# One two-bank PSUM tile for both heads' scores, one VectorE instruction over it, and a new order for the attention and first feed-forward stages

## The chip, the cores and the metric

The kernel runs on one core of one Trainium2 chip. The metric is the device time of one execution in microseconds (us). The core's engines work in parallel from queues of their own: TensorE (PE; PEld is its weight load), VectorE (DVE), ScalarE (ACT), GpSimd (POOL) and SyncE (SP), which here only issues DMAs.

## What is computed

Four batches of 576 tokens with 8 heads of 64. Each head has a pooled ("global") attention over groups of four tokens and a local one over a band of seven; their sum, 2304 tokens by 512, goes through two feed-forward stages:

```python
out_d = sm_attn(q_d, k_d, v_d)            # q, k, v averaged over 4 tokens
out_up = np.repeat(out_d, 4, axis=2)
scores = np.where(np.abs(i - j) < 4, scale * q @ k.T, -1e9)
x = out_up + softmax(scores) @ v          # per head, then heads side by side
h = np.maximum(np.maximum(x @ w1, x @ w2), x @ w3)   # 512 -> 768
x = h @ w_out                                        # 768 -> 512
h = x @ w_in                                         # 512 -> 2048
out = np.maximum(0.01 * h, h) @ w_out2               # 2048 -> 512
```

## The kernel before, in words

All matrices of the feed-forward stages are split into a high and a low part, and each product is three matmuls (high by high, high by low, low by high).

**Units.** The 2304 tokens are eight units of 288 (`NU`, `NCOL`), two per batch. A unit needs its input X (high `xh`, low `xl`); then `L1_mm` makes 18 products of 12 matmuls each (six column blocks by three weights, `ps_h`), `L1_max` keeps the maximum of three (`hm`), `L1_hh` (ScalarE) and `L1_hl` (GpSimd) split it, and `L2_mm` makes four products of 18 matmuls (`ps_o`). Phase 2 (`L3`, `L4`) is the second feed-forward stage; nothing of it is touched.

**Local attention** comes in two ways. For units 0 to 3 (`pairs`) the scores are made by PE for two heads at a time: step C writes two PSUM tiles `ps_ls` (a band mask, then six matmuls), D (VectorE) takes maxima and scales them, E (ScalarE) is six exponentials with sums, H (VectorE) adds an epsilon and inverts, I (GpSimd) normalises, O (PE) transposes into `ps_lt`, o (VectorE) copies to `plt`, P (PE) multiplies by v, Q (VectorE) adds the pooled part (`x`), R (ScalarE) and S (GpSimd) split into X. For units 4 to 7 VectorE, GpSimd and ScalarE do it without PE, each unit in two halves: three products on GpSimd (`qkprod`, line 371), reductions, a mask added on GpSimd (line 391), a subtraction of the maximum on VectorE (line 402), an exponential, a division, three products with v (`pvprod`, line 425) and sums. In unit 4 the probabilities `lp` lie in SBUF, in units 5 to 7 in PSUM (lines 397 to 400). `turn_steps` then transposes the result (`ps_x`), adds the pooled part and splits it into X.

**Pooled attention** (`ds_` steps): A sums groups of four, B is PE's scores `ps_sc` in two tiles, F, G, J, K are the softmax like D, E, H, I; M transposes into two tiles `ps_aT`, m (ScalarE) copies them, N (PE) multiplies by the pooled v (PV, GpSimd), v (ScalarE) copies the result to `up`.

**Weights** of the first stage, 18 `wA` and 6 `wO`, arrive as 64-bit numbers and are converted in four steps: x (ScalarE, lines 304 and 305), y (VectorE, 307 and 310), z (ScalarE, 316) and u (GpSimd, 318). Two work tiles `wy` serve them all. L1 of unit 0 waits for the `wA` one by one, the `ps_o` products for the `wO`.

**The order** is fixed by the program on every engine, and an engine takes its instructions one after the other. The string `ORDER` is the first part, batch 0's attention for unit 0 (each letter a step above, the digit a head pair or a weight); `ps0`, a PSUM pool of eight banks, serves it, with small matmuls on a zero tile `warm` (`fill`) between. From there to the end of phase 1 the class `Plan` sets the order: a list schedule with a cost for each step, due times made from `LEN` (one length per unit) and shifted by kind with `SHIFT`, and a window in which a step may begin (`SLACK`). Its PSUM pools are `mm` (four banks), `at` (two) and `early` (two); `holds` tells it which step takes a buffer and which gives it back.

Of the kernel before, what the change touches and what calls it, by code (L numbers as in the profile page):

```python
# [56 lines left out]
FILL1 = 8  # L57
ON_A = (0, 21, 14)
# [6 lines left out]
SHIFT = {'pv': 31, 'ra': 0, 't': -48, 'mu': 73, 'c': 15, 'ds3': 4, 'ds2': -60, 'pl3': -19, 'pl1': 4}  # L65
SLACK = {'ds1': 100, 'pl3': 150, 'ds3': 30, 'ra': 150, 'pv': 60, 'ds2': 60, 'c': 20, 'mu': 150}
LEN = (64, 78, 40, 47, 39, 56, 39, 39)
# [123 lines left out]
def local_global_attention_moe_kernel(  # L191
# [61 lines left out]
    PS = {"0": tc.alloc_tile_pool(name="ps0", bufs=7, space=PSUM)}  # L253
# [226 lines left out]
    def pl_C(u, h):  # L480
        qr, kr = pl[u, h, "q"], pl[u, h, "k"]
        n = NBLK * KB
        pst = pl[u, h, "ps"] = [scratch(u, "early", "ps_ls") for hh in range(2)]
        if u == 0:
            fill("C", pst[0])
        for t in pst:
            T.matmul(
                out=t[:QB, :n], lhsT=ident_b, rhs=bands[u % 2].rearrange("p n k -> p (n k)"), start=True, stop=False
            )
        for j in range(NBLK):  # L490
            s0 = u % 2 * NCOL + j * QB
            qs, ks = slice(s0, s0 + QB), slice(s0, s0 + KB)
            for hh in range(2):
                rows = slice(64 * hh, 64 * hh + 64)
                T.matmul(  # L495
                    out=pst[hh][:QB, j * KB : j * KB + KB], lhsT=qr[rows, qs], rhs=kr[rows, ks],
# [3 lines left out]
    def pl_D(u, h):  # L500
# [3 lines left out]
        st = pl[u, h, "st"] = [  # L504
            stats[:QB, 24 * h + 6 * hh : 24 * h + 6 * hh + 6] if u == 0 else pst[hh][:QB, n : n + 6] for hh in range(2)
        ]
        for hh in range(2):
            ps = pst[hh][:QB, :n].rearrange("p (n k) -> p n k", n=NBLK)
            V.tensor_reduce(out=st[hh][:, :NBLK], in_=ps, axis=AX.X, op=ALU.max, negate=True)
            V.tensor_scalar(out=nm[:, hh], in0=st[hh][:, :NBLK], scalar1=SCALE, scalar2=None, op0=ALU.mult)  # L510

    def pl_E(u, h):
        n = NBLK * KB
# [7 lines left out]
        for hh in range(2):  # L521
            ps = pst[hh][:QB, :n].rearrange("p (n k) -> p n k", n=NBLK)
            for j in range(NBLK):
                A.activation(  # L524
                    out=et[:, hh, j], in_=ps[:, j], func=AF.Exp, scale=SCALE,
                    bias=nm[:, hh, j : j + 1], accum_out=sm[:, hh, j : j + 1],
                )

    def pl_H(u, h):
        st, sm = pl.pop((u, h, "st")), pl[u, h, "sum"]  # L530
        pl.pop((u, h, "ps"))
        for hh in range(2):
# [8 lines left out]
    def pl_O(u, h):  # L541
        pts = []
        for n, (j0, j1) in enumerate(((0, 2), (2, 3))):
            pt = scratch(u, "at", "ps_lt")
            if u == n == 0:
                fill("O", pt)
            pt = pt[:KB, : (j1 - j0) * 2 * QB].rearrange("p (j h q) -> p j h q", h=2, q=QB)
            for j in range(j0, j1):
                for hh in range(2):
                    T.transpose(out=pt[:, j - j0, hh], in_=pl[u, h, "e"][:, hh, j], identity=ident[:QB, :QB])  # L550
            pts.append(pt)
        pl[u, h, "pt"] = pts
# [747 lines left out]
```

## Time and profile before

| | us |
|---|---|
| median of 3 runs | 841.9 (840.14 to 841.92) |
| the profiled execution | 840.65 |
| its span, first to last instruction | 838.9 |
| PE busy | 809.9 (97%) |
| VectorE, ScalarE, GpSimd busy | 458.0, 401.4, 254.1 |

The profiled execution's time is its span and 1.75 us around it. Lines named L and a number are lines of the kernel before. A time such as 105.02 is counted from the span's start; "a <-b" means that a is written from b. "idle before <-X" says how long the engine stood still and whose work ended that. The view of stretches gives each engine's busy time in a part of the span.

### The profile page before, as it was taken

What the parts mean: (1) busy time and instruction counts of PE and PEld (TensorE: products, weight loads), DVE (VectorE), ACT (ScalarE), POOL (GpSimd) and SP (SyncE); (2) the same over time, 40 slices, a digit from 0 to 9 for tenths busy, and PEclk for the clock granted to TensorE, in tenths of its full rate; (3) what the DMA queues carried; (4) which work ended last, traced back from release to release, by engine and by line L of the source; (5) the groups of instructions that cost most, each with busy time, mean ns of one, the idle gap of its engine ahead of it and who ended that gap; (6) DMA issues with size and microseconds to landing.
All of it is one profiled execution on the core that took longest, in us unless ns stands there. A gap on an engine that the chain in (4) does not pass through costs nothing.

```text
span 838.9 us, 13935 instructions
## 1 busy us (share of the span) xinstructions
PE 809.9 (97%) x5124; PEld 706.6 (84%) x5128; DVE 458.0 (55%) x894; ACT 401.4 (48%) x1451; POOL 254.1 (30%) x237
## 2 busy tenths in 40 slices
PE   7889599989999999999999999999999999999997
PEld 3569499879999999999998888888888888888896
DVE  6769845588886874939509982422232223322332
ACT  5878937678375565137418972322232222322222
POOL 6768749789864792111100000000000000000000
PEclk9989799999999999999999999999999999999999
DMA  9781333435313131242029400300030001000100
GB/s 274 284 341 51 104 119 104 153 125 172 121 52 132 58 88 46 83 135 96 22 73 392 166 0 1 101 0 1 1 101 0 1 1 53 23 1 1 39 13 25
DMA packets 28100, 74.49 MB, mean 89 GB/s; under 512 B 3648, under 2 KB 9152, under 8 KB 28032
## 3 DMA queue, kind: packets, MB, share of 16 engines
q1 hardware_dynamic: 23232, 68.62, 24.1%
q10 hardware_dynamic: 4800, 4.98, 1.7%
q8 instruction: 40, 0.66, 0.3%
q14 instruction: 28, 0.23, 0.1%
HBM read 64.16 MB, written 9.44 MB: 88 GB/s over the span
## 4 chain that ended last, share of the span: by engine, by line
PE 87%; DVE 4%; ACT 4%; DMA 3%; issue 1%; POOL 1%; SPq 0%; ACTq 0%; DVEq 0%; POOLq 0%
PE ps_h L802 26%; PE ps_g L899 24%; PE acc L923 24%; PE ps_o L834 9%; ACT qkprod L385 2%; DMA wA<-in_wa_dram 1%; DMA dsrawv<-in_vP_dram 1%; PE ps_up L717 1%; PE ps_sc L643 1%; DVE lp L402 1%; DVE wl L307 1%; PE ps_aT L695 1%; PE ps_ls L495 1%; PE ps_lo L572 1%; ACT ple L524 1%
## 5 line engine op out<-in xcount | busy, mean ns | idle before, releaser
L802 PE MATMUL ps_h<-xh,wA 128*128 128x288 f32 x1152 | 199.7, 301 | 1.9 <-ACT xh L591 1.8
L923 PE MATMUL acc<-w2o,gh 128*128 128x512 f32 x576 | 177.9, 391 | 0.0
L802 PEld LDWEIGHTS ps_h<-xh,wA 128*128 128x128 f32 x1152 | 167.7, 189 | 7.4 <-issue 2.3
L907 DVE TENSOR_TENSOR g<-g,ps_g 128x512 f32<-128x512 f32 (+1 forms) x80 | 50.7, 634 | 199.7 <-ACT g L906 199.6
L899 PE MATMUL ps_g<-x2h,w2i 128*128 128x512 f32 (+1 forms) x640 | 159.0, 370 | 0.1
L906 ACT ACTIVATE g<-ps_g 128x512 f32<-128x512 f32 (+1 forms) x80 | 44.5, 556 | 200.7 <-PE ps_g L899 200.7
L899 PEld LDWEIGHTS ps_g<-x2h,w2i 128*128 128x128 f32 x640 | 114.6, 188 | 23.3 <-ACT ev L841 0.3
L923 PEld LDWEIGHTS acc<-w2o,gh 128*128 128x128 f32 x576 | 107.0, 188 | 22.0
L923 PE MATMUL acc<-w2o,gl 128*128 128x512 f32 x288 | 112.0, 391 | 0.0
L802 PE MATMUL ps_h<-xl,wA 128*128 128x288 f32 x576 | 109.4, 296 | 0.5 <-POOL xl L594 0.5
L802 PEld LDWEIGHTS ps_h<-xl,wA 128*128 128x128 f32 x576 | 88.3, 189 | 0.7 <-POOL xl L594 0.7
L834 PE MATMUL ps_o<-hh,wO 128*128 128x288 f32 x384 | 81.4, 306 | 0.0
L899 PE MATMUL ps_g<-x2l,w2i 128*128 128x512 f32 (+1 forms) x320 | 79.6, 370 | 0.0
L371 POOL TENSOR_TENSOR qkprod<-lq,lk 128x1344 f32<-128x1344 f32 x24 | 73.8, 3081 | 6.5 <-ACT qkprod L385 3.7
L825 POOL TENSOR_TENSOR hl<-hm,hh 128x288 fp32r<-128x288 f32 x48 | 41.3, 861 | 108.3 <-ACT hh L821 108.0
L818 DVE TENSOR_TENSOR hm<-hm,ps_h 128x288 f32<-128x288 f32 x96 | 43.3, 451 | 56.3 <-PE ps_h L802 51.3
L911 DVE TENSOR_TENSOR gl<-g,gh 128x512 fp32r<-128x512 f32 (+1 forms) x80 | 51.0, 638 | 39.6 <-ACT gh L910 35.6
L385 ACT ACTIVATE qkprod<-qkprod 128x64 f32<-128x64 f32 x280 | 67.4, 250 | 3.8 <-POOL qkprod L371 2.8
L910 ACT ACTIVATE gh<-g 128x512 fp32r<-128x512 f32 (+1 forms) x80 | 47.0, 588 | 42.2 <-DVE g L907 41.8
L899 PEld LDWEIGHTS ps_g<-x2l,w2i 128*128 128x128 f32 x320 | 56.8, 188 | 10.9
L834 PEld LDWEIGHTS ps_o<-hh,wO 128*128 128x128 f32 x384 | 62.9, 193 | 2.0 <-issue 1.6
L923 PEld LDWEIGHTS acc<-w2o,gl 128*128 128x128 f32 x288 | 54.1, 188 | 11.8
(129 smaller groups left out, 1110.6 us busy)
## 6 DMA issues: line engine op xcount, KB each, us to landing
sqk<-in_qk_dram SPq DMA_DIRECT2D x20, 579.0 KB, 4.2
wA<-in_wa_dram SPq DMA_DIRECT2D x18, 512.0 KB, 10.5
w2i<-in_w_in_dram SPq DMA_DIRECT2D x16, 512.0 KB, 6.0
w2o<-in_w_out_dram SPq DMA_DIRECT2D x16, 512.0 KB, 8.5
dsrawv<-in_vP_dram SPq DMA_DIRECT2D x16, 320.0 KB, 4.2
x2d<-ev ACTq DMA_DIRECT2D x32, 144.0 KB, 1.7
raw<-x2d SPq DMA_DIRECT2D x16, 256.0 KB, 3.9
lk<-in_kL_dram SPq DMA_DIRECT2D x8, 480.0 KB, 4.1
```

The lines of the kernel that those rows point to most:

```text
L371: P.tensor_tensor(out=pr, in0=in0, in1=in1, op=ALU.mult)
L385: A.activation(out=pr[:, r, j], in_=pr[:, r, j], func=AF.Copy, accum_out=sc[:, r, j : j + 1])
L802: T.matmul(out=ps, lhsT=wA[m, e][wi][:, kk * 128 : kk * 128 + 128], rhs=xx[:, kk] if u < PEU else xx[:, :, kk, :], start=n == 0, stop=n == ...
L818: V.tensor_tensor(out=hmax[u, m], in0=hmax[u, m], in1=ps, op=ALU.max)
L825: P.tensor_tensor(out=hl[:, m], in0=hmax[u, m], in1=hh[:, m].bitcast(F32), op=ALU.subtract)
L834: T.matmul(out=ps, lhsT=wO[m][wi][:, os_], rhs=xx[:, m], start=m == n == 0, stop=m == M1 - 1 and n == 2)
L899: T.matmul(out=ps, lhsT=w2i[m][wi][:, kk * 128 : kk * 128 + 128], rhs=xx[:, kk, :n], start=j == 0, stop=j == 3 * KC - 1,)
L906: A.activation(out=g, in_=ps, func=AF.Copy, scale=0.01)
L907: V.tensor_tensor(out=g, in0=g, in1=ps, op=ALU.max)
L910: A.activation(out=gh, in_=g, func=AF.Copy)
L911: V.tensor_tensor(out=gl, in0=g, in1=gh.bitcast(F32), op=ALU.subtract)
L923: T.matmul(out=accs[c, t], lhsT=a[:, ts], rhs=w, start=m == 0 and j == 0, stop=m == M2 - 1 and j == 2)
```

## The change

Wherever a step used two one-bank PSUM tiles for two heads (or two halves), it now uses one tile of two banks, and the VectorE or ScalarE instructions that read them work on both banks at once: D, H, F and J have two instructions instead of four, o and m one instead of two. N moves from the `at` pool to `mm`. `turn_steps` takes the nine rows of a unit in groups of eight and one, where it took three groups. `ORDER` is a new string, and `SHIFT`, `SLACK`, `LEN` and the plan's costs are new, so that phase 1 is ordered anew. Eight matmuls on the zero tile (`FILL2`) stand in unit 0's first product, ahead of the part that needs the last head pair.

```diff
 ORDER = (
-    "C0 A0 A1 B0 L0 D0 C1 A2 E0 F0 L1 B1 H0 G0 D1 I0 C2 J0 E1 F1 K0 A3 L2 G1 M0 D2 x0 O0 J1 m0 L3 y0 "
...
+    "C0 A0 A1 L0 B0 D0 C1 A2 E0 F0 L1 B1 H0 G0 D1 I0 A3 E1 C2 F1 L2 x0 H1 O0 J0 D2 G1 K0 y0 E2 L3 B2 o0 J1 "
...
+FILL2 = 8
...
-LEN = (64, 78, 40, 47, 39, 56, 39, 39)
+LEN = (58, 68, 44, 42, 51, 58, 39, 40)
...
     def scratch(first, kind, name):
...
-            return PS["0"].tile([128, 512], F32, tag=tag, bufs=6 if tag == "b" else 1, name=name)
-        return PS[kind].tile([128, 512], F32, tag=kind, name=name)
+            if tag == "b":
+                return PS["0"].tile([128, 2, 512], F32, tag=tag, bufs=3, name=name)
+            return PS["0"].tile([128, 512], F32, tag=tag, bufs=1, name=name)
+        return PS[kind].tile([128, 512] if kind == "mm" else [128, 2, 512], F32, tag=kind, name=name)
...
     def pl_D(u, h):
...
-        for hh in range(2):
-            ps = pst[hh][:QB, :n].rearrange("p (n k) -> p n k", n=NBLK)
-            V.tensor_reduce(out=st[hh][:, :NBLK], in_=ps, axis=AX.X, op=ALU.max, negate=True)
-            V.tensor_scalar(out=nm[:, hh], in0=st[hh][:, :NBLK], scalar1=SCALE, scalar2=None, op0=ALU.mult)
...
+        V.tensor_reduce(
+            out=st[:, :, :NBLK], in_=pst[:QB, :, :n].rearrange("p h (n k) -> p h n k", n=NBLK), axis=AX.X,
+            op=ALU.max, negate=True,
+        )
+        V.tensor_scalar(out=nm, in0=st[:, :, :NBLK], scalar1=SCALE, scalar2=None, op0=ALU.mult)
...
     def pl_H(u, h):
...
+        V.tensor_scalar(out=st[:, :, NBLK : 2 * NBLK], in0=sm, scalar1=1e-9, scalar2=None, op0=ALU.add)
+        V.reciprocal(out=sm, in_=st[:, :, NBLK : 2 * NBLK])
...
     def pl_o(u, h):
...
-        for (j0, j1), pt in zip(((0, 2), (2, 3)), pl.pop((u, h, "pt"))):
-            V.tensor_copy(out=t[:, j0:j1], in_=pt)
+        V.tensor_copy(out=t, in_=pl.pop((u, h, "pt"))[:KB, :, :NCOL])
...
     def ds_N(b, h):
-        ps = scratch(b, "at", "ps_up")
+        ps = scratch(b, "mm", "ps_up")
...
     def turn_steps(u):
...
-        groups = ((0, 3), (3, 7), (7, 9)) if half and not whole else ((0, 4), (4, 8), (8, 9))
+        groups = ((0, 8), (8, 9))
...
     def L1_mm(u, m, e):
...
         for n, (wi, xx, kk) in enumerate(order):
+            if u == m == e == 0 and n == 3 * (KC - 1):
+                fill("", PS["early"].tile([128, 2, 512], F32, tag="early", name="warm_ps"), FILL2)
...
-        PS["at"] = p1.enter_context(tc.tile_pool(name="ps_at", bufs=2, space=PSUM, reuse_waits="tile"))
-        PS["early"] = tc.alloc_tile_pool(name="ps_early", bufs=2, space=PSUM, reuse_waits="tile")
+        PS["at"] = p1.enter_context(tc.tile_pool(name="ps_at", bufs=1, space=PSUM, reuse_waits="tile"))
+        PS["early"] = tc.alloc_tile_pool(name="ps_early", bufs=1, space=PSUM, reuse_waits="tile")
```

D, H, F, J, ds_B, ds_M, pl_C and pl_O change alike: the index of the head becomes the tile's second dimension. Three places of the new order follow.

**VectorE, end of batch 0.** `x32` is step Q of the second, third and fourth head pair, `plt` step o, `wl3` and `wy` the two halves of a conversion's step y; the names `wA1_1` and so on say which weight. Before:

```order
L307 SCALAR_TENSOR_TENSOR wl3_611<-wA0_1_150,wl3_611 128x512
L310 SCALAR_TENSOR_TENSOR wy_610<-wy_610,wl3_611 128x512
L585 TENSOR_TENSOR x32_647<-ps_lo_618,up_410 128x288
L560 COPY plt_661<-ps_lt_635 102x384
L560 COPY plt_661<-ps_lt_642 102x192
L307 SCALAR_TENSOR_TENSOR wl3_650<-wA2_0_166,wl3_650 128x512
L310 SCALAR_TENSOR_TENSOR wy_649<-wy_649,wl3_650 128x512
L585 TENSOR_TENSOR x32_684<-ps_lo_667,up_410 128x288
L307 SCALAR_TENSOR_TENSOR wl3_681<-wA1_2_164,wl3_681 128x512
```

Now:

```order
L310 SCALAR_TENSOR_TENSOR wl3_571<-wA0_2_156,wl3_571 128x512
L313 SCALAR_TENSOR_TENSOR wy_570<-wy_570,wl3_571 128x512
L559 COPY plt_600<-ps_lt_580 102x576
L586 TENSOR_TENSOR x32_620<-ps_lo_605,up_432 128x288
L310 SCALAR_TENSOR_TENSOR wl3_617<-wA1_0_160,wl3_617 128x512
L313 SCALAR_TENSOR_TENSOR wy_616<-wy_616,wl3_617 128x512
L310 SCALAR_TENSOR_TENSOR wl3_629<-wA2_1_168,wl3_629 128x512
L313 SCALAR_TENSOR_TENSOR wy_628<-wy_628,wl3_629 128x512
L310 SCALAR_TENSOR_TENSOR wl3_636<-wA2_0_166,wl3_636 128x512
```

The last Q had six conversions ahead of it and has five now; the copy is one instruction.

**PE, unit 0's first product and the first C of unit 1.** `ps_h` is the product, `warm_ps` the new small matmuls, `ps_ls` step C; the brackets name the semaphores that a row waits for. Before:

```order
L802 MATMUL ps_h<-xh,wA_0_393 128x288 [waits Activation_49]
L802 MATMUL ps_h<-xl,wA_0_393 128x288 [waits Pool_49]
L802 MATMUL ps_h<-xh,wA_0_393 128x288
L487 LDWEIGHTS ident_b
L487 MATMUL ps_ls<-band,ident_b 96x306 [waits PE_49]
L487 LDWEIGHTS ident_b
L487 MATMUL ps_ls<-band,ident_b 96x306 [waits DVE_49]
L495 MATMUL ps_ls<-sqk 96x102 x6
L802 MATMUL ps_h<-xh,wA_1_645 128x288
```

Now (the pair of `warm` rows comes eight times):

```order
L803 MATMUL ps_h<-xh,wA_0_421 128x288
L289 LDWEIGHTS warm [waits DVE_49]
L289 MATMUL warm_ps<-warm 128x512 [waits Activation_49]
L289 LDWEIGHTS warm
L289 MATMUL warm_ps<-warm 128x512
...
L803 MATMUL ps_h<-xh,wA_0_421 128x288 [waits Activation_49]
L803 MATMUL ps_h<-xl,wA_0_421 128x288 [waits Pool_49]
L803 MATMUL ps_h<-xh,wA_0_421 128x288
L490 LDWEIGHTS ident_b
L490 MATMUL ps_ls<-band,ident_b 96x306 [waits PE_49]
```

VectorE's step that C's second bank waited for is the eighth conversion's y (of weight `wA2_1`). The small matmuls wait for the eighth conversion's y now too (of `wA2_0`), because their tile has both banks, and the last three matmuls of the product stand behind them.

**GpSimd, around unit 4's second mask addition** (`ls`). `qkprod` are the products of local attention, `ple` step I, `xl` step S, `hl` the split of h. Before:

```order
L391 TENSOR_TENSOR ls<-ls,mask_66 128x21
L825 TENSOR_TENSOR hl<-hm,hh 128x288
L539 TENSOR_TENSOR ple<-ple,plsm 96x612
L391 TENSOR_TENSOR ls<-ls,mask_66 128x21
L594 TENSOR_TENSOR xl<-x_2244,xh 128x288
L371 TENSOR_TENSOR qkprod<-lq,lk 128x1344 x2
```

Now:

```order
L541 TENSOR_TENSOR ple<-ple,plsm 96x612
L394 TENSOR_TENSOR ls<-ls,mask_66 128x21
L374 TENSOR_TENSOR qkprod<-lq,lk 128x1344 x2
L826 TENSOR_TENSOR hl<-hm,hh 128x288
L595 TENSOR_TENSOR xl<-x_2159,xh 128x288
L541 TENSOR_TENSOR ple<-ple,plsm 96x612
L374 TENSOR_TENSOR qkprod<-lq,lk 128x1344
```

The two products that follow the second mask addition stood one S behind it and now stand right behind it.

## Rows read from the trace of the kernel before

**Rows 1.** The page: busy time of each engine, share of the span, instructions.

```profile
PE 809.9 (97%) x5124; PEld 706.6 (84%) x5128; DVE 458.0 (55%) x894; ACT 401.4 (48%) x1451; POOL 254.1 (30%) x237
```

**Rows 2.** Busy time in three stretches (windows), by engine, with granted clock.

```profile
core 0: us, PE busy (x) PEld busy (x) DVE busy (x) ACT busy (x) POOL busy (x), PEclk, DMA share, GB/s
45.70:102.10 56.40, 44.02 (x350) 39.18 (x349) 46.03 (x119) 48.26 (x152) 40.09 (x37) 0.86 0.46 168
88.30:105.00 16.70, 8.18 (x75) 6.12 (x75) 14.26 (x45) 14.56 (x51) 11.79 (x11) 0.65 0.24 83
436.80:838.90 402.10, 396.98 (x1824) 328.94 (x1824) 155.98 (x251) 141.14 (x252) 0.00 (x0) 1.00 0.14 51
```

**Rows 3.** Waits of PE: total us, times, longest us.

```profile
PE ps_ls L487 <- DVE ps_ls L534: 5.6, 1, 5.6
PE ps_up L717 <- DVE plt L560: 3.1, 1, 3.1
PE ps_ls L487 <- DVE wy L310: 1.6, 1, 1.6
```

**Rows 4.** Timeline of PE, 17 to 51 us: start, us, instruction, idle before.

```profile
17.87 3.42 PE L286 MATMUL warm_ps<-warm 128*128 128x512 bf16 x8
50.88 0.41 PE L487 MATMUL ps_ls<-band,ident_b 96*96 96x306 bf16 x1 [1.63 <-DVE wy L310]
```

**Rows 5.** Chain of waits, fifteen equal matmuls, three stretches: start, us, what.

```profile
105.02 3.01 PE ps_o L834 x15
172.27 3.47 PE ps_o L834 x15
261.17 2.00 PE ps_o L834 x15
```

**Rows 6.** Groups of VectorE instructions by shape: count, busy us, mean ns, idle before.

```profile
L381 DVE TENSOR_REDUCE ls<-qkprod 128x21 f32<-128x1344 f32 x8 | 12.2, 1544 | 0.0
L509 DVE TENSOR_REDUCE ps_ls<-ps_ls 96x3 f32<-96x306 f32 x24 | 11.4, 473 | 4.5 <-PE ps_ls L495 4.5
L560 DVE COPY plt<-ps_lt 102x384 f32<-102x384 f32 x16 | 8.8, 551 | 6.6 <-PE ps_lt L550 4.5 <-POOL dsvaT L475 2.1
L381 DVE TENSOR_REDUCE ls<-qkprod 128x7 f32<-128x448 f32 x8 | 4.9, 614 | 3.9 <-POOL qkprod L371 3.9
L510 DVE TENSOR_SCALAR plnm<-ps_ls 96x3 f32<-96x3 f32 x24 | 3.8, 157 | 0.8
L310 DVE SCALAR_TENSOR_TENSOR wy<-wy,wl 128x512 int32<-128x512 int32 x56 | 39.6, 708 | 2.9
```

**Rows 7.** Timeline of VectorE in the first batch and at the last conversions.

```profile
24.55 0.82 DVE L560 COPY plt<-ps_lt 102x384 f32<-102x384 f32 x2 [2.09 <-POOL dsvaT L475]
45.24 0.45 DVE L585 TENSOR_TENSOR x<-ps_lo,up 128x288 f32<-128x288 f32 x1
...
101.41 0.69 DVE L310 SCALAR_TENSOR_TENSOR wy<-wy,wl 128x512 int32<-128x512 int32 x1
```

**Rows 8.** Timeline of ScalarE: end of a conversion, one begun, six exponentials.

```profile
84.19 0.62 ACT L316 ACTIVATE wA<-wy 128x512 fp32r<-128x512 f32 x1
84.71 0.66 ACT L304 ACTIVATE wy<-wO 128x512 f32<-128x512 f32 x1
85.82 0.34 ACT L524 ACTIVATE ple<-ps_ls,plnm 96x102 f32<-96x102 f32 x1
87.75 0.67 ACT L304 ACTIVATE wy<-wO 128x512 f32<-128x512 f32 x1
```

**Rows 9.** GpSimd: the fifth output-weight conversion; the two products at 161.74.

```profile
103.16 1.28 POOL L318 TENSOR_TENSOR wO<-wy,wO 128x512 fp32r<-128x512 f32 x1 [0.71 <-ACT wO L316]
...
161.74 6.07 POOL L371 TENSOR_TENSOR qkprod<-lq,lk 128x1344 f32<-128x1344 f32 x2
```

**Rows 10.** VectorE line L402's and L425's durations: min/median/max ns.

```profile
L402 DVE TENSOR_TENSOR lp<-ls,lp x8: 225/228/6598, 159.5 to 327.8; 128x63 f32<-128x63 f32 x8
...
L425 DVE TENSOR_TENSOR pvprod<-lp,lv x24: 1532/1550/2712, 176.8 to 350.5; 128x1344 f32<-128x1344 f32 x24
```

More of the change, by code (lines that the diff above doesn't have):

```diff
@@ L495, in pl_C @@
                 T.matmul(
-                    out=pst[hh][:QB, j * KB : j * KB + KB], lhsT=qr[rows, qs], rhs=kr[rows, ks],
+                    out=pst[:QB, hh, j * KB : j * KB + KB], lhsT=qr[rows, qs], rhs=kr[rows, ks],
                     start=False, stop=j == NBLK - 1,
@@ L541, in pl_O @@
     def pl_O(u, h):
[L542 to L552, printed above, removed]
+        pt = scratch(u, "at", "ps_lt")
+        if u == 0:
+            fill("O", pt)
+        for j in range(NBLK):
+            for hh in range(2):
+                T.transpose(
+                    out=pt[:KB, hh, j * QB : j * QB + QB], in_=pl[u, h, "e"][:, hh, j], identity=ident[:QB, :QB]
+                )
+        pl[u, h, "pt"] = pt
     def pl_o(u, h):
         if u == 0:
-            t = late_tile([KB, NBLK, 2, QB], "plt")
+            t = late_tile([KB, 2, NCOL], "plt")
         else:
-            t = pools[u // 2].tile([KB, NBLK, 2, QB], F32, tag="plt", bufs=1, name="plt")
-        for (j0, j1), pt in zip(((0, 2), (2, 3)), pl.pop((u, h, "pt"))):
-            V.tensor_copy(out=t[:, j0:j1], in_=pt)
+            t = pools[u // 2].tile([KB, 2, NCOL], F32, tag="plt", bufs=1, name="plt")
+        V.tensor_copy(out=t, in_=pl.pop((u, h, "pt"))[:KB, :, :NCOL])
         pl[u, h, "aT"] = t
@@ L636, in ds_B @@
         t = dst[b, h, "qk"]
-        pst = dst[b, h, "ps"] = [scratch(b, "at", "ps_sc") for hh in range(2)]
+        pst = dst[b, h, "ps"] = scratch(b, "at", "ps_sc")
         if b == 0:
-            fill("B", pst[0])
+            fill("B", pst)
         for c in range(2):
@@ L675, in ds_J @@
         dst.pop((b, h, "ps"))
[L676 to L679 removed]
+        sm = sum4.rearrange("p (h n) -> p h n", h=2)
+        V.tensor_scalar(out=st[:, :, 2:4], in0=sm, scalar1=1e-9, scalar2=float(FAC), op0=ALU.add, op1=ALU.mult)
+        V.reciprocal(out=sm, in_=st[:, :, 2:4])
     def ds_norm(b, h):
@@ L1021, in pairs @@
             go(f"S{k}", "POOL", 0.8, lambda: pl_S(u, h), [f"R{k}"])
-            for n in range(2):
-                holds("early", 2, f"C{k}", [f"H{k}"])
-                holds("at", 2, f"O{k}", [f"o{k}"])
+            holds("early", 1, f"C{k}", [f"H{k}"])
+            holds("at", 1, f"O{k}", [f"o{k}"])
             holds("mm", 4, f"P{k}", [f"Q{k}"])
@@ L1182, in local_global_attention_moe_kernel @@
         for b in range(B):
-            last = [f"ta{2 * b + 1}.2"] if 2 * b + 1 >= PEU else [f"Q{2 * b + 1}.{h}" for h in range(4)]
+            last = [f"ta{2 * b + 1}.1"] if 2 * b + 1 >= PEU else [f"Q{2 * b + 1}.{h}" for h in range(4)]
             holds("up", 2, f"v{b}.0" if b else "L0.0", last)
@@ L1190, in open3 @@
             open_p2a()
-        go("open3", "SP", 0.0, open3, [f"tx{NU - 1}.2", f"L{NU - 2}.0"] + [f"v{B - 1}.{h}" for h in range(4)])
+        go("open3", "SP", 0.0, open3, [f"tx{NU - 1}.1", f"L{NU - 2}.0"] + [f"v{B - 1}.{h}" for h in range(4)])
         first = base + 12
```

159 lines of the change are left out of this document (75 added, 84 removed), and 6 rows, old and new, of the table ORDER.

## Prediction

> **What bounds the kernel now.** I read the page first: PE is busy 97% of the span [rows 1], so a change can win only what PE waits, and what it does at its lower clock. The view by stretches says where that is. Phase 2, the last 402.1 us, has PE at work for 397.0 at full granted clock [rows 2]; the change leaves its code alone, and I carry it over unchanged. The loss lies ahead of it. PE's waits name it: 5.6 us for VectorE's step H, 3.1 for step o, 1.6 for a weight conversion [rows 3]. The first stands between 88.3 and 105.0, where PE is busy for 8.2 of 16.7 us and its granted clock is 0.65 [rows 2]. The reader should see that VectorE (14.3) and ScalarE (14.6) are both nearly full there. They are converting the output weights, and the fifth of these is ready only when GpSimd's step, begun at 103.16 and 1.28 long, ends at 104.44 [rows 9]; the `ps_o` products that need it begin at 105.02 [rows 5]. So from about 45 to 105 us the supply of converted weights, shared with unit 1's softmax steps, sets the end, and PE's waits are its shadow. Over 45.7 to 102.1 ScalarE is busy for 48.3 of 56.4 us and VectorE for 46.0 [rows 2]: neither is full, they pass work to each other, and ScalarE is slightly the fuller.
>
> After 105 us PE has one real loss more, the 3.1 us for step o, which follows a subtraction on VectorE that took 6.60 us instead of 0.23 [rows 3, 10].
>
> **VectorE's instructions.** A reduction of 1344 elements takes 1.544 us and one of 448 takes 0.614 [rows 6], so 1.04 ns an element. D's reduction of 306 takes 0.473, hence one of 612 about 0.473 + 306 x 0.00104 = 0.79. D was 2 x (0.473 + 0.157) = 1.26 and becomes 0.79 + 0.157 = 0.95: 0.31 saved. H was four small instructions, 4 x 0.157 = 0.63, and becomes 0.31: another 0.31. F and J have the same form and I give them the same prices. Step o was 0.551 and, by the slope, 0.35 for the smaller copy; one copy of 576 is 0.551 + 192 x 0.00104 = 0.75: 0.15 saved. That is 0.77 us for each of 16 pair steps and 0.62 for each of 16 pooled steps, 22 us of VectorE's 458. Most of it buys nothing: from 105 us on PE is the bound, and VectorE's work lies beside PE's. It counts where weights are converted.
>
> **The first batch, to the last Q at 45.24** [rows 7]. Up to 24.55 nothing moves: step o of the first head pair waits there for GpSimd's pooling of the fourth v, whose load is where it was. From there to the last Q, VectorE's list was five conversions, two F, two J, three H, one D, four o, four Q; now it is four conversions, two F, three J, two H, one D, four o, four Q. With 2 x 0.708 = 1.42 for a conversion [rows 6] the saving is 1.42 for that and 3.1 for the rest: 4.5 at most. At least it is what ScalarE is relieved of, one conversion less: 1.11 + 0.52 = 1.63 (begun at 84.71 to the next instruction at 85.82; last step 84.19 to 84.71) [rows 8]. The two engines hand their results to each other there, so I take a value between, **-2.5** (bounds -1.6 and -4.5).
>
> **The eight small matmuls.** They wait for the eighth conversion, as half of C did until 50.88 [rows 4]. Eight of them took 3.42 us at 17.87 [rows 4], which is 0.43 each, what 512 columns take at the lower of PE's two clocks (1.2 GHz); after a wait I expect that again. Ahead of them PE idles, as before; behind them the product's last three matmuls and C are that much later. What hides it: from there to the `ps_o` products PE has 17 products of 12 matmuls at 2.00/15 = 0.133 us each [rows 5], 27 us, and 15 attention steps. Before, it was busy for 44.0 us there, partly at the lower clock, with nearly the same products and steps [rows 2]; without that I estimate 39. From 55 us it ends near 94, ahead of the converted weights. So I price them at 0. If the weights came by 94, they would cost up to 3.4.
>
> **From there to the fifth output weight.** I count VectorE's instructions between the fourth Q and that weight's y in both orders. Before: 17 conversions, six D, five H, two F, two J, two o, six pooling reductions of 576 (about 0.75 by the slope), two Q. Now: 18 conversions, five D, four H, one F, one J, four o, four poolings, three Q. The 12 maxima stay. With the prices above this is 44.8 against 40.2: 4.6 us less, though the extra conversion is in it. On ScalarE one E goes (85.82 to 87.75, 1.93 [rows 8]) and one G (four exponentials to E's six, about 1.3), against one more conversion (1.63) and one rounding of x (at most 0.5): 1.1 us less. So -1.1 if ScalarE binds alone, -4.6 if VectorE does; they take turns, and I take **-3.0**.
>
> **The clock behind the wait.** Fifteen `ps_o` matmuls took 3.01 us at 105.02 and 2.00 later on [rows 5]: with the idle time ahead of them shorter, that **-1.0** should come back (bounds 0 and -1.0).
>
> **Unit 4's subtraction.** Its 6.60 us [rows 10] span the two products that GpSimd ran from 161.74 for 6.07 us [rows 9]; PE lost 3.1 us by it and then did fifteen matmuls in 3.47 instead of 2.00 [rows 3, 5]: 4.6 in all. In the new order two products stand right behind the second mask addition, so VectorE's subtraction, which waits for that addition, meets them again unless VectorE is late. But step H, o and D beside it are shorter, and PE has two whole `ps_o` rounds at that point. I take **-1.5** (bounds 0, the same again, and -4.6, all gone).
>
> The Trainium skill, page "SBUF — State Buffer", section "Who interferes with whom", says that a VectorE instruction with two SBUF inputs contends with a GpSimd instruction that reads SBUF, and that whoever comes second blocks altogether. By that rule this term is 0 and the sum 834.1. The trace agrees where unit 4 is concerned: one subtraction of eight took 6.60 us, the median 0.228 [rows 10].
>
> **The two-bank tiles** cost waits in principle: a bank can no longer be refilled while its neighbour is read. But C, B, O and M each took both banks of their pool before too, so at the most one VectorE instruction's length is lost where PE waits for it, under 0.8 us, and I put 0. N leaves `at`, which frees it. The transposes in groups of eight take one round of 8 rows where two overlapped; each has some 20 to 30 `ps_o` matmuls beside it, 3 to 4 us, which hides them. The last conversions for phase 2 are ordered no later than before. 0 for all of these, with +2 as the bound.
>
> **The sum** is made against the profiled execution: 840.65 - 2.5 - 3.0 - 1.0 - 1.5 = 832.65, so **832.6 us**. The median shown is 841.9, 1.25 above that execution and within the spread of the three; I leave the forecast where the sum puts it. About 0.2% (1.7 us) is what a measurement here can tell from no change.
>
> **Rivals.**
>
> 1. *More than that.* All bounds on the good side: 840.65 - 4.5 - 4.6 - 1.0 - 4.6 = 826. For it speaks that VectorE is named by most of PE's waits; against it that ScalarE, busy for 48.3 of 56.4 us, is hardly relieved. Chance 0.12.
>
> 2. *ScalarE binds, nothing moves.* Only 1.6 + 1.1 are won and the small matmuls give 2 back, because PE comes late to unit 0 and is itself the bound to the first `ps_o`: about 840. For it speaks ScalarE's load; against it PE's 39 us of work in a stretch of over 45. Chance 0.12.
>
> 3. *Slower: unit 4's products with v lie under GpSimd's.* In the new order GpSimd starts unit 4's products right at the first `ps_o`, some 25 us earlier in the program, and unit 5's follow while VectorE does unit 4's six products with v, which also take both inputs from SBUF. One such already took 2.71 us for 1.55 [rows 10]. If each met one product (6.07 / 2 = 3.04), VectorE would be held for 18 us. At the rate of before (4.6 lost for 6.4 held) PE loses 13, in place of 4.6. With half of the first two terms and the clock's 1.0 that is 840.65 + 8.4 - 2.75 - 1.0 = 845.3. The point from which it decides: over 15 us of holds, as (6.5 + 4.6) / 0.72. Against it: VectorE has been relieved by 0.77 us a pair step in the same stretch. Chance 0.16.
>
> That the change does not do what it says (a two-bank instruction costing as much as two) would leave rival 2's time; it is counted there.
>
> **How the numbers follow.** The forecast keeps 0.60, with a range of its own from 828 to 838. The whole range, **824 to 842**, takes in rivals 1 and 2 and leaves out most of rival 3 and what is beyond the bounds. Faster by over 0.2%: the forecast, rival 1 and a third of rival 2, **0.76**. Within: the rest of rival 2, **0.08**. Slower: rival 3, **0.16**.
>
> **What would show it.** Right: D's reduction near 0.79 us and half as many; the last Q near 43; the `ps_o` products at 98 to 101, with full clock within a few matmuls; PE's busy time ahead of phase 2 unchanged but for the clock; phase 2 at 402 us, beginning near 429. The small matmuls should begin right after the eighth y, near 49, at 0.43 us each. Wrong: the last Q still at 45 or later (ScalarE binds the first batch); `ps_o` still at 105; PE waits over 4 us after 105 for H or o, with `pvprod` at over 2.5 us; or a phase 2 of another length.

## The result and the profile after

The changed kernel takes **848.6 us** (median of 4, 847.8 to 849.6) against 841.3 of the kernel before (median of 4): a ratio of 1.0089, 95% interval 1.0071 to 1.0107. It is slower by 0.9%, where 832.6 us (824 to 842) were forecast.

The profiled execution took 849.57 us. Its page and its stretches, which answer to [rows 1, 2], with phase 2 last (columns: stretch, its length, busy time and instructions of PE, PE's weight loads, VectorE, ScalarE and GpSimd, granted clock, DMA share, GB/s):

```profile
PE 812.7 (96%) x5131; PEld 708.3 (84%) x5136; DVE 443.3 (52%) x748; ACT 400.2 (47%) x1431; POOL 253.7 (30%) x237
```

```profile
20.00:40.00 20.00, 13.88 (x96) 8.04 (x98) 7.83 (x19) 10.40 (x41) 11.75 (x12) 0.74 0.84 298
100.00:120.00 20.00, 13.69 (x116) 11.78 (x116) 11.79 (x28) 13.43 (x47) 16.71 (x13) 0.83 0.41 150
160.00:200.00 40.00, 34.78 (x279) 31.74 (x279) 34.52 (x41) 19.74 (x125) 26.80 (x19) 0.87 0.34 102
445.60:847.80 402.20, 397.02 (x1824) 328.99 (x1824) 156.01 (x251) 141.22 (x252) 0.00 (x0) 1.00 0.14 51
```

Two of these stretches in the kernel before:

```profile
20.00:40.00 20.00, 18.36 (x162) 10.43 (x162) 15.64 (x53) 16.12 (x62) 13.32 (x13) 0.96 0.81 295
160.00:200.00 40.00, 36.71 (x316) 33.41 (x315) 34.17 (x67) 27.02 (x178) 36.27 (x28) 0.96 0.39 132
```

Phase 2 is 402.2 us long, as before. VectorE is busy for 14.7 us less. All of the loss lies ahead of phase 2, which begins at 445.61 instead of 436.76, 8.85 us late. The reader should see the first row: between 20 and 40 us every engine does less than before, VectorE half, at a granted clock of 0.74 instead of 0.96. No engine is full there; all of them wait.

VectorE's groups by shape (columns as in [rows 6]) show that the prices were right:

```profile
L559 DVE COPY plt<-ps_lt 102x576 f32<-102x576 f32 x16 | 11.9, 747 | 9.2 <-POOL dsvaT L478 5.9 <-PE ps_lt L549 3.3
L512 DVE TENSOR_REDUCE ps_ls<-ps_ls 96x6 f32<-96x612 f32 x12 | 9.5, 792 | 2.2 <-PE ps_ls L498 2.1
L516 DVE TENSOR_SCALAR plnm<-ps_ls 96x6 f32<-96x6 f32 x12 | 1.9, 159 | 0.4
```

D's reduction takes 0.792 us (0.79 was worked out), step o 0.747 (0.75). (Added up over all groups, VectorE's durations fall by 21.0 us, about the 22 forecast; its busy time falls by 14.7, since rows that follow each other overlap at their ends, more often before.) But the first row says as well that VectorE sat idle for 5.9 us ahead of one step o, until GpSimd had pooled the fourth v. Before, that wait was 2.09 [rows 7]. VectorE's, GpSimd's and PE's timelines around it, in this order (start, us, instruction, idle before it and what ended it):

```profile
19.57 0.69 DVE L313 SCALAR_TENSOR_TENSOR wy<-wy,wl 128x512 int32<-128x512 int32 x1
26.19 0.76 DVE L559 COPY plt<-ps_lt 102x576 f32<-102x576 f32 x1 [5.93 <-POOL dsvaT L478]
...
27.33 0.76 DVE L657 TENSOR_REDUCE stats<-ps_sc 72x4 f32<-72x576 f32 x1
...
34.35 0.46 DVE L586 TENSOR_TENSOR x<-ps_lo,up 128x288 f32<-128x288 f32 x1 [3.98 <-ACT up L726]
...
49.90 0.46 DVE L586 TENSOR_TENSOR x<-ps_lo,up 128x288 f32<-128x288 f32 x1 [1.48 <-PE ps_lo L573]
```

```profile
24.09 1.26 POOL L477 TENSOR_TENSOR dsrawv<-dsrawv 72x512 f32<-72x512 f32 x1 [2.12 <-DMA dsrawv<-in_vP_dram]
25.43 0.72 POOL L478 TENSOR_TENSOR dsvaT<-dsrawv 72x256 f32<-72x256 f32 x1
```

```profile
22.71 0.66 PE L695 MATMUL ps_aT<-ident,dsqke 72*72 72x72 f32 x8
27.00 1.01 PE L289 MATMUL ps_lo<-warm 128*128 128x512 bf16 x2 [3.62 <-DVE plt L559]
27.94 1.23 PE L573 MATMUL ps_lo<-plt,sv 102*64 102x96 f32 x12
...
38.84 0.72 PE L573 MATMUL ps_lo<-plt,sv 102*64 102x96 f32 x12
...
57.32 0.61 PE L289 MATMUL warm_ps<-warm 128*128 128x512 bf16 x1 [6.15 <-DVE wy L313]
...
110.30 0.85 PE L835 MATMUL ps_o<-hh,wO 128*128 128x288 f32 x2
```

Step o writes into the buffer from which GpSimd reads the fourth v, so it cannot begin before 26.15. PE's next instruction, P's fill, needs o; PE idles 3.62 us, and most of what it then does up to 37 us runs at half speed (P 1.23 us instead of 0.72). The last Q begins at 49.90 instead of 45.24, the eighth conversion ends at 57.3, the eight small matmuls follow it, and the output products begin at 110.30 instead of 104.95.

The second loss is in unit 4. GpSimd, VectorE and PE there:

```profile
160.44 6.08 POOL L374 TENSOR_TENSOR qkprod<-lq,lk 128x1344 f32<-128x1344 f32 x2
...
174.08 3.04 POOL L374 TENSOR_TENSOR qkprod<-lq,lk 128x1344 f32<-128x1344 f32 x1
```

```profile
160.87 7.07 DVE L428 TENSOR_TENSOR pvprod<-lp,lv 128x1344 f32<-128x1344 f32 x1
...
173.27 3.93 DVE L418 TENSOR_TENSOR lp<-lp,lsm 128x63 f32<-128x63 f32 x1
```

```profile
171.87 0.43 PE L490 MATMUL ps_ls<-band,ident_b 96*96 96x306 bf16 x2 [3.39 <-ACT lp L410]
```

A product with v of 1.55 us takes 7.07, and ends 1.42 us after GpSimd's second product. The profile puts PE's 3.39 us wait down to ScalarE's `lp`; but C needs the one `early` tile, and H, which frees it, stood behind the held product on VectorE and ended at 171.72.

### The profile page after: what moved, and what is told of

Same layout as the page of the kernel before. It is cut to its first block, busy times and chain, and to the rows that moved or that the text cites. A ratio compares the mean times of both kernels' runs of the same rounds, so it can differ in the third digit from the quotient of the medians.

```text
span 847.8 us, 13740 instructions
## 1 busy us (share of the span) xinstructions
PE 812.7 (96%) x5131; PEld 708.3 (84%) x5136; DVE 443.3 (52%) x748; ACT 400.2 (47%) x1431; POOL 253.7 (30%) x237
## 4 chain that ended last, share of the span: by engine, by line
PE 88%; DVE 5%; DMA 3%; ACT 2%; issue 1%; POOL 1%; SPq 0%; DVEq 0%; ACTq 0%; POOLq 0%
PE ps_h L803 26%; PE ps_g L900 24%; PE acc L924 23%; PE ps_o L835 8%; DMA dsrawv<-in_vP_dram 2%; PE ps_up L717 1%; DMA sv<-in_vW_dram 1%; PE ps_aT L695 1%; PE ps_sc L644 1%; DVE pvprod L428 1%; DVE wl L310 1%; PE ps_ls L498 1%; DVE wy L313 1%; ACT ple L528 1%; PE ps_lo L573 1%
## 5 line engine op out<-in xcount | busy, mean ns | idle before, releaser
L900 PEld LDWEIGHTS ps_g<-x2h,w2i 128*128 128x128 f32 x640 | 114.6, 188 | 23.3 <-ACT ev L842 0.3
```

Source lines behind the costliest of these rows:

```text
L900: T.matmul(out=ps, lhsT=w2i[m][wi][:, kk * 128 : kk * 128 + 128], rhs=xx[:, kk, :n], start=j == 0, stop=j == 3 * KC - 1,)
```

## The experiments

In all of them the kernel before was timed on the same chip. Its median was 842.4 us beside runs 1 to 4, 841.4 beside 5 to 8, 840.7 beside 9 to 12 and 841.9 beside 13 to 15, so runs of different groups are better compared by their ratios than by their medians. Positions are from each run's profiled execution (one), in us; phase 2 is 401.9 to 402.7 long in all of them.

| run | kernel | median us | ratio to before (95%) | o starts | last Q | output products | phase 2 |
|---|---|---|---|---|---|---|---|
| | before | 841.3 | | 24.55 | 45.24 | 104.95 | 436.76 |
| | changed | 848.6 | 1.0089 (1.0071 to 1.0107) | 26.19 | 49.90 | 110.30 | 445.61 |
| 1 | old order of first batch | 841.4 | 0.9991 (0.9978 to 1.0004) | 23.84 | 43.95 | 102.79 | 436.67 |
| 2 | no small matmuls | 846.6 | 1.0049 (1.0033 to 1.0066) | 25.28 | 50.43 | 109.35 | 444.41 |
| 3 | before, new order alone | 847.4 | 1.0052 (1.0034 to 1.0069) | 25.61 | 49.14 | 111.22 | 443.40 |
| 4 | old constants | 854.4 | 1.0140 (1.0123 to 1.0158) | 23.31 | 47.07 | 113.31 | 450.01 |
| 5 | o further back | 846.6 | 1.0052 (1.0035 to 1.0070) | 24.35 | 46.27 | 106.66 | 442.00 |
| 6 | buffer of its own for o | 842.5 | 0.9999 (0.9980 to 1.0018) | 19.90 | 42.70 | 103.65 | 439.56 |
| 7 | old order, no small matmuls | 841.0 | 0.9998 (0.9982 to 1.0013) | 24.85 | 44.76 | 102.64 | 437.80 |
| 8 | 7, unit 4's lp in PSUM | 840.9 | 0.9986 (0.9971 to 1.0002) | 23.51 | 45.13 | 108.02 | 436.70 |
| 9 | 7, unit 5's products held back | 834.3 | 0.9926 (0.9905 to 0.9948) | 24.19 | 43.97 | 101.49 | 431.55 |
| 10 | 9 and 6's buffer | 833.7 | 0.9913 (0.9896 to 0.9929) | 21.05 | 44.58 | 101.52 | 431.17 |
| 11 | 6, no small matmuls, held back | 835.7 | 0.9941 (0.9926 to 0.9956) | 19.49 | 41.40 | 100.27 | 430.00 |
| 12 | before, held back | 842.8 | 1.0020 (1.0011 to 1.0030) | 24.72 | 45.42 | 104.60 | 439.66 |
| 13 | 6, no small matmuls | 840.9 | 0.9990 (0.9975 to 1.0005) | 19.48 | 41.29 | 100.25 | 434.89 |
| 14 | 6 once more | 842.9 | 1.0015 (0.9997 to 1.0032) | 19.21 | 45.78 | 106.26 | 441.69 |
| 15 | changed, held back | 843.0 | 1.0010 (0.9995 to 1.0026) | 25.23 | 51.69 | 112.04 | 439.83 |

### Which part of the change

Run 1 puts the old order string into the changed kernel, run 3 the new one into the kernel before; run 2 sets the small matmuls to none, run 4 the three tables of phase 1 to those of before (the strings and tables stand in the diff of the change).

```diff
-    "C0 A0 A1 L0 B0 D0 C1 A2 E0 F0 L1 B1 H0 G0 D1 I0 A3 E1 C2 F1 L2 x0 H1 O0 J0 D2 G1 K0 y0 E2 L3 B2 o0 J1 "
+    "C0 A0 A1 B0 L0 D0 C1 A2 E0 F0 L1 B1 H0 G0 D1 I0 C2 J0 E1 F1 K0 A3 L2 G1 M0 D2 x0 O0 J1 m0 L3 y0 "
...
```

> The changed kernel with the first batch in the order of before; two-bank tiles, eight small matmuls and the new constants of phase 1 stay. Theory A (the new order of the first batch loses the time: step P of the first head pair stands on TensorE ahead of work that does not need GpSimd's fourth v, so three engines stop together): the last Q comes back from 49.9 to 43 to 45 us, the first output products from 110.3 to 105 to 107, and the time to 843 to 845. Theory B (the loss is made in phase 1, by tiles of which one is all there is and by the new constants; the first batch is hidden by the conversion of weights anyway): the last Q comes earlier just the same, but the first output products stay at 109 or later, and the time at 847 to 849.

> The kernel before with the new order of the first batch alone: one-bank tiles, no eight small matmuls, the old constants of phase 1. Theory A: the wait for GpSimd's fourth v costs it the same, last Q at 49 to 50 us and the time 845 to 847. Theory B: last Q late too, but the time at 841 to 842.5, since weights set the first output products.

Theory A came out on run 1's last Q (43.95), and the output products came earlier still than it expected, 102.79; the time, 841.4, is better than its 843 to 845. Run 3 costs the kernel before 0.5% with one-bank tiles and old constants, its median 847.4 just above what A expected. The new order of the first batch is the loss. Without it the change is even with before, not faster.

```diff
-FILL2 = 8
+FILL2 = 0
```

> The changed kernel without its eight small matmuls ahead of the last three of unit 0's first product; nothing else. Theory A: TensorE waits 6.7 us in 99.6 to 108.4 for conversions and step H, which is more than the 3.4 us of the small matmuls, so they are hidden: 847.5 to 849.5, first output products within 0.7 us of 110.3. Rival (they lie on the path, since TensorE comes late to unit 0): 844.5 to 846, first output products near 107.

The medians say 2.0 us off (the ratios 3.4), the profile only 0.95 at the output products, and o was 0.91 earlier there. Neither reading settled it; runs 13 and 14 do, below.

> The changed kernel with the three tables of phase 1 (shifts, slacks, lengths) of before; new first batch, tiles and small matmuls stay. Theory A: only what unit 4 lost goes back, up to 3.5 us: 845 to 848, first output products still at 109 or later. Theory B: 842 to 844, with no product of the step with v over 2.8 us in unit 4 and the first output products at 106 to 108.

Both theories missed: slower by 5.8 us in the medians, 4.3 by the ratios. PE's waits in this run begin, after the small matmuls' own, with

```profile
PE ps_lt L549 <- DVE dssum L681: 5.1, 1, 5.1
PE ps_aT L695 <- DVE dssum L681: 3.2, 1, 3.2
```

Both are steps that need the one two-bank `at` tile, and J, which frees it, is late. So the tables belong to the tiles; the two cannot be judged apart.

### What in the first batch

Run 5 moves o on VectorE alone; run 6 gives o a buffer that GpSimd does not read.

```diff
-  L3 B2 o0 J1 M0 F2 x1 K1 P0 H2 G2 I1 y1 ...
+  L3 B2 J1 M0 F2 x1 K1 H2 G2 I1 o0 P0 y1 ...
```

> The changed kernel with step o of the first head pair moved on VectorE behind J of the second pooled head and F and H of the third (TensorE's list stays as it is). Theory A1 (what stands behind the waiting o is the cost): these three and ScalarE's steps behind them run in the 5.9 us in which VectorE idled, last Q at 45 to 47 us, time 843.5 to 846. Rival A2 (TensorE's own list is the cost: P of the first pair stands ahead of the rest there, whatever VectorE does): last Q at 49 or later, time 847 to 849.5.

```diff
-            t = late_tile([KB, 2, NCOL], "plt")
+            t = pools[0].tile([KB, 2, NCOL], F32, tag="plt0", bufs=1, name="plt") if h == 0 else late_tile([KB, 2, NCOL], "plt")
```

> The changed kernel with a buffer of its own for the first head pair's transposed probabilities, so that step o need not wait until GpSimd has read the fourth v out of that buffer; every order stays. If that wait makes the loss of the first batch: o starts at 20 to 21 us instead of 26.2, the last Q ends at 43 to 45, and the time is 842 to 844. Rival (the new order is longer by itself, wherever o starts): last Q at 48 or later, time 846.5 to 849.

Run 6 met its first expectation: o at 19.90, last Q at 42.70, 842.5 us. One buffer undoes 6 us with every order left as it is, so most of the loss comes from that wait. Over the profiled executions of the new order the last Q lies at 46.3 to 51.7 where o waits (the changed kernel, runs 2 to 5 and 15) and at 41.3 to 45.8 where it has its buffer (6, 11, 13, 14); in the old order it lies at 44.0 to 45.4. Whether the new order has a price besides is taken up with run 11. Run 5 moved the last Q back as A1 expected (46.27), but its 846.6 us lie between the two theories: what stands behind o on VectorE is part of the cost, and most of it remains with PE's list as it is.

Runs 13 and 14 are that kernel without and with the small matmuls.

> The sixth run's kernel (changed kernel, step o with a buffer of its own) without the eight small matmuls. If they are on the path: 1.5 to 2.5 us under the fourteenth run, first output products at 101 to 102 instead of 103.7. If the conversions of weights hide them: within 0.8 us of the fourteenth run, first output products within 0.6 us of its own.

> The sixth run's kernel once more, as the other half of this comparison on one chip: 841.5 to 843.5.

The times differ by 2.1 us (the intervals overlap a little). From the last Q to the output products it takes 58.9 to 59.0 us in all new-order runs with the new constants and no small matmuls (runs 2, 11, 13) and 60.4 to 61.0 in those with them (the changed kernel and runs 5, 6, 14, 15). So the eight cost **1.5 us**; they are on the path.

Run 14 also shows what the first batch's time hangs on besides. It is run 6's kernel, o was even earlier, and yet its last Q came 3.1 us later. Two stretches of run 6, then of run 14, and the second P in each on PE's timeline:

```profile
22.00:26.00 4.00, 2.21 (x25) 1.35 (x24) 2.00 (x6) 2.89 (x11) 3.80 (x4) 1.00 1.03 326
26.00:30.00 4.00, 4.00 (x38) 2.21 (x35) 2.11 (x4) 1.38 (x3) 4.00 (x5) 1.00 1.02 414
...
30.67 0.72 PE L573 MATMUL ps_lo<-plt,sv 102*64 102x96 f32 x12
```

```profile
22.00:26.00 4.00, 2.22 (x25) 1.35 (x24) 1.72 (x4) 3.06 (x12) 3.92 (x5) 0.99 1.03 348
26.00:30.00 4.00, 4.00 (x23) 2.55 (x23) 1.22 (x2) 1.54 (x5) 4.00 (x4) 0.50 1.03 420
...
33.52 1.23 PE L573 MATMUL ps_lo<-plt,sv 102*64 102x96 f32 x12
```

The granted clock stayed at 1.00 in the one and fell to 0.50 (1.2 of 2.4 GHz) in the other. The first batch is a chain that passes through PE, so its steps at half speed lengthen it.

### What in unit 4

Run 7 joins runs 1 and 2. Run 8 puts unit 4's `lp` into a PSUM bank, taken from the four of the products.

> The changed kernel with the first batch in the order of before and without the eight small matmuls: what is left of the change is the two-bank tiles and the constants of phase 1. From the 841.4 of the run with the old order, the 2.0 us that the small matmuls cost in the second run should come off: 838.5 to 840.5. Rival (with the old order TensorE is early enough to hide them): 841 to 842.

```diff
-            pb = pools["att"].tile([128, n + 2 * RU], F32, tag="lp", bufs=2, name="lp")
+            if i % 2 == 0:
+                loc["lp4"] = PS["l4"].tile([128, 512], F32, tag="l4", name="lp")
+            pb = loc["lp4"][:, 128 * (i % 2) : 128 * (i % 2) + n + 2 * RU]
...
-        PS["mm"] = p1.enter_context(tc.tile_pool(name="ps_mm", bufs=4, space=PSUM, reuse_waits="tile"))
+        PS["mm"] = p1.enter_context(tc.tile_pool(name="ps_mm", bufs=3, space=PSUM, reuse_waits="tile"))
+        PS["l4"] = p1.enter_context(tc.tile_pool(name="ps_l4", bufs=1, space=PSUM, reuse_waits="tile"))
...
```

> The same, and unit 4's softmax scores (lp) in a PSUM bank instead of SBUF, as units 5 to 7 have them; the products get three banks instead of four for it. If the hold of VectorE by GpSimd's products is what costs unit 4 its time: all six products with v take 1.5 to 1.6 us instead of up to 7.07, TensorE's idle 5 us at 150 to 180 us go, and the time is 833 to 836.5. Rival (the bank given up costs as much): 839 to 842, with TensorE waiting over 4 us in all for maxima or copies of its products to free a bank.

Run 7 stayed at 841.0, its rival's value: the output products begin 2.3 us earlier than before, and unit 4 takes it back. In run 8 the hold is gone, as the minimum, median and maximum of its 24 products with v show beside those of the changed kernel:

```profile
L430 DVE TENSOR_TENSOR pvprod<-lp,lv x24: 1522/1546/1557, 154.8 to 332.0; 128x1344 f32<-128x1344 f32 x24
```

```profile
L428 DVE TENSOR_TENSOR pvprod<-lp,lv x24: 1512/1549/7069, 154.7 to 352.5; 128x1344 f32<-128x1344 f32 x24
```

From the output products to phase 2 it needs 328.7 us instead of run 7's 335.2: 6.5 us won. The rival's time came out too: the output products come 5.4 us later, and the time does not move. Its reason did not: PE waits 2.4 us in all for maxima and copies of the products, where it said over 4. The longest wait, 4.55 us ahead of the output products, is for J, which frees the one `at` tile. (The bank and the order that the planner makes of three banks were changed together; which of them cost it was not tried.)

Run 9 leaves `lp` in SBUF and makes GpSimd wait instead.

```diff
         V.tensor_tensor(out=pr, in0=in0, in1=in1, op=ALU.mult)
         loc[i, "pv", c] = pr
+        if i == I0 + 1 and c == RU // RC - 1:
+            P.tensor_copy(out=pools["att"].tile([128, 1], F32, tag="gate", bufs=1, name="gate"), in_=pr[:, 0, 0, 0:1])
...
-                go(f"mu{i}.{c}", "POOL", 3.08, ..., [f"lq{i}", f"lk{i}"] + ([f"mu{i}.{c - 1}"] if c else []))
+                go(f"mu{i}.{c}", "POOL", 3.08, ..., [f"lq{i}", f"lk{i}"] + ([f"mu{i}.{c - 1}"] if c else [f"pm{I0 + 1}.{RU // RC - 1}"] if u == PEU + 1 else []))
```

> The seventh run's kernel (old order of the first batch, no small matmuls, two-bank tiles and new constants) with unit 5's products of q and k held back on GpSimd until VectorE's last product with v of unit 4 is done, by a GpSimd instruction of one element that reads it. If those products, by holding VectorE, cost unit 4 its time: no pvprod over 2 us before 210 us, no idle stretch of TensorE over 1 us at 140 to 200, start of phase 2 from 437.8 to 431 to 433, time 834 to 837. Rival (the work put off is late for unit 5, or GpSimd's queue stands still): 839 to 843, with TensorE waiting for unit 5's or 6's steps after 230.

It came out as expected: 834.3 us, phase 2 at 431.55. PE's waits between 120 and 440 us are now these two, of which one is phase 2's own first (ahead of the output products, at 99.55, C still waits 4.67 us for H):

```profile
PE ps_x L758 <- DVE xl L790: 1.5, 1, 1.5
PE ps_g L902 <- ACT ev L844: 1.0, 1, 1.0
```

Runs 10, 11, 12 and 15 put the same edit elsewhere.

> The same, and the first head pair's transposed probabilities in a buffer of their own, as in the sixth run. If step o's wait for the fourth v sets the first batch in the old order too, the last Q moves from 44.8 to 41 to 43, the first output products to 100 to 102, and the time is 1 to 3 us under the ninth run's. Rival (conversions of weights hide it): no difference over 0.8 us.

> The changed kernel (new order of the first batch) with three edits: the buffer of its own, no small matmuls, and unit 5's products held back. From the sixth run's 842.5, the hold gives 5 to 6 and the small matmuls up to 2: 834 to 838, about as the tenth run. If the new order has a price beyond step o's wait, it stays over 1.5 us behind the tenth run.

> The kernel before with unit 5's products held back in the same way and nothing else: one-bank tiles, old order, old constants. Its hold was one subtraction of 6.60 us that cost TensorE 4.6 us: 836.5 to 838 if nothing else moves. If the two-bank tiles save time in phase 1 beyond that, this run is 1.5 to 3 us slower than the ninth; if not, they are within 1 us of each other.

> The changed kernel with unit 5's products held back behind unit 4's products with v, and nothing else. If unit 4's hold is worth the 6.5 us that the ninth run won over the seventh, wherever unit 4 begins: 841 to 843, no pvprod over 2 us before 215. If the loss of the first batch leaves VectorE more time there, so that the hold costs only the 3.5 us by which its stretch is longer than before's: 844 to 846.

Run 10, 833.7, is the fastest median here, 0.9% under before; against run 9 the buffer brings nothing that can be told apart (0.6 us), so in the old order o's wait is covered. Run 11's median is 1.9 us behind run 10's, more than the 1.5 that its expectation named as the sign of a price of the new order. But the intervals just overlap, with four executions each, and its profiled execution begins phase 2 1.2 us earlier; run 13 against run 7 shows no price either (0.9990 and 0.9998). Whether the new order costs anything once it is freed of its wait is not settled. Run 15 wins 5.6 us over the changed kernel by the medians, 6.6 by the ratios, so the hold was worth that there, nearer to the first of its two expectations (though one product with v, at 156.49, still took 2.15 us).

Run 12 missed: the hold went (its longest product with v is 1.558 us) and the time did not fall. The stretch from 240 to 280 us in run 12 and in run 9 shows one difference:

```profile
240.00:280.00 40.00, 39.14 (x294) 37.72 (x294) 38.02 (x66) 28.20 (x191) 31.25 (x25) 1.00 0.33 110
```

```profile
240.00:280.00 40.00, 39.91 (x311) 38.98 (x310) 30.67 (x50) 28.80 (x182) 28.50 (x21) 1.00 0.28 92
```

Unit 5's work put off meets a VectorE that is busy for 38.0 of 40 us with one-bank instructions and for 30.7 with two-bank ones. That this is the reason is argued, not shown: the two runs also differ in the planner's tables, and in this stretch PE stands idle for only 0.9 us in run 12 (0.1 in run 9); its longest wait after 120 us is 2.35, for VectorE's split of X, at 359.86. What is shown is that the tiles with their tables alone (run 7) and the products held back alone (run 12) win nothing, and both together 0.7% (run 9).

## Why the prediction was wrong

In the profiled executions its steps and what they came to, in us; the measured sum is the 8.85 by which phase 2 begins late.

| step | forecast | measured |
|---|---|---|
| first batch, to the last Q | -2.5 | +4.7 |
| eight small matmuls | 0 | +1.5 |
| from there to the output products | -3.0 | -0.8 |
| the clock behind the wait and unit 4 | -2.5 | +3.5 |

**The first batch** is where it failed, at "Up to 24.55 nothing moves" and at the count behind it. The sum of VectorE's instructions was right, but VectorE does not bound that stretch; a chain over four engines does. All that the shorter instructions saved ahead of o was idled away, 5.93 us instead of 2.09, since o's start is set by a DMA and GpSimd. The fourth v came 1.6 us later as well, its load unchanged in the program (o starts between 23.3 and 26.2 in the runs where it needs that v: a spread of the transfers). And the order had changed: VectorE's J of the second pooled head, and ScalarE's m and PE's N of the first, had stood ahead of the wait and now stood behind it. PE idled, the clock fell, and its ten groups of matmuls from 27.0 to 37.1 us took 10.0 us, where the same groups at full clock later in the batch give 6.0 (P's 1.23 for 0.72 is one). The sign that I had given for this, the last Q still at 45 or later, came true, but not for its reason: ScalarE is busy for only 10.4 of the 20 us there. I had read each engine's list between the right two points, but asked only how much stood there, not what stood behind the one step that waits.

**The small matmuls** I priced at 0 with a bound of 3.4; the way from the last Q to the output products, with them and without (run 13 and those named with it), gives 1.5. The cover I named for them, PE's work from 55 to 94, was itself late.

**From there to the output products** the count was right, but it ended at the wrong step. I counted VectorE's list to the fifth output weight's y. That y begins 54.86 us after the last Q, where it was 56.17 [rows 7]: 1.3 us less with the small matmuls in it, 2.8 without them, and 2.7 in run 13. But PE waits for that weight in neither kernel. Before, it came to the products from M and P, and M had waited for step o, which stands right behind that y on VectorE:

```profile
102.71 1.15 PE L695 MATMUL ps_aT<-ident,dse 72*72 72x72 f32 x8 [1.21 <-DVE plt L560]
```

Now C stands ahead of the products and waits for H, which VectorE reaches only after a Q, two pooling reductions and F. VectorE (the y, and H), then GpSimd (the fifth weight is the second of the two) and PE:

```profile
104.76 0.69 DVE L313 SCALAR_TENSOR_TENSOR wy<-wy,wl 128x512 int32<-128x512 int32 x1
...
107.92 0.15 DVE L536 TENSOR_SCALAR ps_ls<-plsm 96x6 f32<-96x6 f32 x1
```

```profile
106.37 2.50 POOL L321 TENSOR_TENSOR wO<-wy,wO 128x512 fp32r<-128x512 f32 x2 [1.96 <-ACT wO L319]
```

```profile
108.35 0.74 PE L490 MATMUL ps_ls<-band,ident_b 96*96 96x306 bf16 x2 [4.63 <-DVE plsm L537]
```

From the y to the products it takes 5.54 us instead of 3.54, and 5.5 in runs 1, 6, 7, 9 and 13 too: two of the 3.0 us are lost behind the point where I stopped counting. (The sum was off besides: by the prices given, with 0.45 for a Q [rows 7], the list before comes to 45.8, not 44.8, so the bound was -5.6.) Nor did the clock's -1.0 come back, with 4.63 us of idle time ahead of C: the first fifteen products take 2.76 us instead of 2.92.

**Unit 4** went as rival 3 described, at a smaller size: the products did meet, VectorE was held for 5.5 us at 160.87, 3.7 at 173.27 and 1.2 at 202.08, 10.4 in all where I had asked for 15 before it would decide (before, 6.4 and 1.2 by [rows 10]). C waited twice, 3.39 us up to 171.87 and 1.83 up to 182.50, for an H that stood behind a held instruction (it ended at 171.72 and 182.35); before, PE had waited there once, for 3.1. I gave it 0.16 by itself and did not put it together with the first batch. The Trainium skill, page "SBUF — State Buffer", section "Who interferes with whom", says that a VectorE instruction with at most one SBUF input, outside its two-port modes, does not contend with GpSimd, and that one with two SBUF inputs contends with a GpSimd instruction that reads SBUF. The trace agrees on both: in run 8, with `lp` in PSUM, the product with v begun at 154.76 takes 1.55 us beside one of GpSimd's that runs from 154.56 for 3.09, and with `lp` in SBUF one takes 7.07. The term of -1.5, which I took against that rule, should have been 0 or worse.

Right were the prices of the two-bank instructions, the length of phase 2, and the count of VectorE's list up to the fifth weight's y. What is shown by an edit: the order, o's buffer, the small matmuls' price and the hold. What is only argued: how the 3.0 us behind o split between the clock and the queues, and, from the rows alone, that C's wait for H ahead of the output products costs the two us there.

## What to carry to other kernels

Where queues are in order, ask of each reordered list which step waits for something that cannot move (a load, another engine's last read of a shared buffer) and what now stands behind it; work saved ahead of such a step was worth nothing here, and a buffer of its own gave 6 us back. Count a list up to the step for which the next engine really waits, and not up to the result that it is meant to supply. Relief of an engine that does not bind won no time by itself; it did once GpSimd's products were held back as well. The planner's timing did not keep the two engines apart; a dependency did.

## What the runs showed of the hardware

A held VectorE instruction was not let in between two GpSimd products in a row: at 160.87 it waited for both (6.08 us) and ended 1.42 us after the second. It goes the other way too. Further on in the changed kernel a GpSimd subtraction took 3.72 us, where it takes 0.79 to 0.82 alone, beside two products of VectorE:

```profile
182.20 3.72 POOL L595 TENSOR_TENSOR xl<-x,xh 128x288 fp32r<-128x288 f32 x1 [5.08 <-ACT xh L592]
```

```profile
182.28 2.98 DVE L428 TENSOR_TENSOR pvprod<-lp,lv 128x1344 f32<-128x1344 f32 x2
```

I had also not expected one kernel's first batch to differ by 3.1 us between two executions. In runs 6 and 14 PE was busy for 2.21 and 2.22 of the 4 us from 22 to 26, with its idle time in like portions, and the clock of the next 4 us was 1.00 in the one and 0.50 in the other.
